# The last three blocks of a filter's forward transform as three fp16 products instead of one fp32 product

## The chip, the cores and the metric

The kernel runs on one core of a Trainium2 chip. The metric is the device time of one execution in microseconds, as the median of several runs; the span is the time from the first to the last instruction of one profiled execution.

## What is computed

Two parts share the core, and their results stand side by side in the output. A is attention with 16 heads of 28 columns and one key and value head (2048 rows, 448 columns). B is a global filter: a real two-dimensional FFT, a product with a complex weight, and the way back.

```
q = (x @ wq).reshape(B, S, 16, 28);  k = x @ wk;  v = x @ wv        # S = 2048, D = 448
p = softmax(q k^T * 28 ** -0.5);     a = (p v) @ wo
X = rfft2(B_x);  X = X * (w_r + 1j * w_i);  b = irfft2(X, (S, D))
out = concatenate([a, b], -1)
```

## The kernel before

A planner orders the first 60 us (projections, keys, the first query tile, and blocks 0 to 3 of the filter's first part). Then comes the loop over the attention, 16 groups (a chunk of 512 rows, four heads) of 16 steps. A step is: TensorE makes two pairs of score tiles (`scores`, four fp16 matmuls of 32 rows for each tile), ScalarE exponentiates each pair in one instruction of 128x1024 (`p`), and TensorE multiplies the result with the values (`values`, four fp32 matmuls). Scores use three double banks of PSUM, the values' sums one of two further banks, in turn by group; `group_out` copies a group's sum out on VectorE and so frees its bank.

Everything else of TensorE is cut into units that `fill` puts between steps, into the bank of the two that the current group does not use: the filter's blocks 5 to 7, later the third part of the filter (`z_unit`, `y_unit`), and the output product (`w_unit`, L1196). The order is fixed when the program is built, by a clock that adds estimated durations (`clk`, `after(when, duration, function)`), so each engine's instructions stand in one row and an instruction that has to wait holds up all that stand behind it.

The filter's first part works on eight blocks q of 256 columns. For each: VectorE folds the input by sums and differences (`fold_part`: `late["x", q]` to `late["f", q]`, 113x1024); `late_features` multiplies with the cosines `cs1` (units q, p with p = 0, 1: 16 fp32 matmuls of 113 columns, L173), VectorE copies the result to `late["a", q]` (L1013); `late_points` multiplies with the twiddles `late["w", q]` (8 fp32 matmuls of 226 columns, L1026), VectorE copies to `bs` (L1035) and SP stores it (`t1`). Blocks 0 to 3 are done by the planner, the features of block 4 too; the points of block 4 and blocks 5 to 7 are late units of the loop. When the last is stored, `spectrum` loads all points of the spectrum back (X), and VectorE alone runs the 32-point transforms, the weights and the way back for some 200 us, which opens the third part.

Two numbers are needed on every partition as a scale: `bounce` stores a column of maxima to DRAM (`md`), loads it back broadcast to all partitions (`mw`), and after 14 us by the clock VectorE reduces `mw` and computes the scales. Before the change this happens twice: early for the values' and the output weight's scale (`largest`; `m`, `scales`), which the first `group_out` needs, and once for the filter's third part (`mx`). `weight_top` loads the filter's weight eight times for a maximum.

The tiles `spoh` and `spol` are the four spare tiles that hold the blocks' data until the output product needs them; `banks` is all of PSUM, `vs` the values, `ka` the keys, `qt`, `qh`, `ql`, `qd`, `qa` the query tile of the next group on its way through DRAM, `woh` and `wol` the high and low half of the output weight.

Of the kernel before, what the change touches and what calls it, by code (L numbers as in the profile page):

```python
# [12 lines left out]
F32 = mybir.dt.float32  # L13
# [88 lines left out]
def kernel(ctx: ExitStack, tc: tile.TileContext, t: dict):  # L102
# [29 lines left out]
    def spin(*dims):  # L132
        return view(bank[next(turn) % 6], *dims)
# [9 lines left out]
    for (n, q), x in late.items():  # L143
        dims = {"x": dict(k=4, n=256), "f": dict(k=4, j=4, h=2, m=32), "w": dict(h=2, j=4, m=64), "a": dict(j=2, e=2, n=226)}[n]
        late[n, q] = x.rearrange(f"p ({' '.join(dims)}) -> p {' '.join(dims)}", **dims)
    xb, ff = {}, {}
# [20 lines left out]
    def features(pa, f, p):  # L167
        for e in range(2):
            for k in range(2):
                for h in range(2):  # L170
                    for r in range(2):
                        r0 = 64 * h + 32 * r
                        mm(pa[r0:r0 + 32, e, 113 * k:113 * k + 113], f[:113, 2 * r + k, 2 * p + e, h], cs1[:113, 2 * r + k],  # L173
                           start=True, stop=True)
# [24 lines left out]
    def late_load(q, names):  # L199
        for n in names:  # L200
            nc.sync.dma_start(late[n, q], t["xb"][q] if n == "x" else t["fz"][:, q - L])
# [30 lines left out]
    with tc.tile_pool(name="f1", bufs=2) as f1[0], tc.tile_pool(name="w1", bufs=1) as w1, ExitStack() as ctx1:  # L232
# [234 lines left out]
        def late_start():  # L467
            late_load(5, "xw")
            late_load(6, "xw")
            late_load(4, "w")  # L470
# [148 lines left out]
        def tops():  # L619
# [115 lines left out]
    def after(when, dur, f, *a):  # L735
        heapq.heappush(events, (when, next(serial), dur, f, a))
# [172 lines left out]
    def bounce(m, then):  # L909
        d = dp.tile([128, 2], F32, name="md", bufs=2)  # L910
        nc.sync.dma_start(d, m[:, :2])
        w = ap.tile([128, 128, 2], F32, name="mw", bufs=1)
        nc.sync.dma_start(w, d.rearrange("(o a) b -> o a b", o=1).to_broadcast([128, 128, 2]))

        def go():
            V.tensor_reduce(m[:, :2], w.rearrange("p a b -> p b a"), axis=AX.X, op=ALU.max)
            V.tensor_scalar(m[:, :2], m[:, :2], 1e-30, None, op0=ALU.max)
            then(m)
        after(clk["dve"] + 14.0, 1.0, go)
# [75 lines left out]

    def late_fold(q, part=0):
        fold_part(late["x", q][:113], late["f", q][:113], part)
        if part < 2:
            after(clk["dve"], (1.22, 1.4)[part], late_fold, q, part + 1)
        else:  # L1000
            if q == 6:
                late_load(7, "x")
            work["l"].extend([late_features(q, 0), late_features(q, 1)])

    def late_features(q, p):
        def go(b):
            features(view(bank[b], 2, 226), late["f", q], p)
            after(clk["pe"] + LAG, 0.6, out, b)
            if q < 7 and p:
                after(clk["pe"] + (1.8 if q == 5 else 5.0), 1.22, late_fold, q + 1)  # L1010

        def out(b):
            V.tensor_copy(late["a", q][:, p], view(bank[b], 2, 226))  # L1013
            free[b] = clk["dve"] + 0.1
            after(clk["dve"] + 0.2, 0.0, work["l"].appendleft, late_points(q, p))
        return 0.86, go

    bsl = {}

    def late_points(q, p):  # L1020
        def go(b):
            pb = view(bank[b], 2, 226)
            for h in range(2):
                for e in range(2):
                    for m in (0, 32):
                        mm(pb[64 * e + m:64 * e + m + 32, h], late["w", q][:, h, 2 * p + e, m:m + 32], late["a", q][:, p, e],  # L1026
                           start=True, stop=True)
            after(clk["pe"] + LAG, 0.6, out, b)
            if q == 6 and p:
                late_load(7, "w")  # L1030

        def out(b):
            if p == 0:
                bsl[q] = fp.tile([128, 2, 2, 2, 113], F32, name="bs")
            V.tensor_copy(bsl[q][:, :, :, p], view(bank[b], 2, 2, 113))  # L1035
# [7 lines left out]
        return 0.76, go  # L1043
# [337 lines left out]
def _constants():  # L1381
# [41 lines left out]
    c["fw"], c["fz"] = fw[:, :16], fz.reshape(128, 4, 2, 4, 64)  # L1423
    c["fi"] = np.stack([rot(2 * np.pi * (np.outer(kp, n1) / 64 + n2 * kp[:, None] / S)) for n2 in range(32)], 1)
    c = {k: np.ascontiguousarray(v.astype(f)) for k, v in c.items()}
    for k, scale in (("fi", 64.0), ("cs3", 32.0 * D)):
        x = c[k] * f(scale)
        h = x.astype(np.float16)
        c[k] = np.ascontiguousarray(np.stack([h, (x - h.astype(f)).astype(np.float16)], 2))
# [68 lines left out]
```

## Time and profile before

| | |
|---|---|
| median of 3 runs (lowest, highest) | 579.97 us (579.77, 580.02) |
| the profiled execution: time, span | 579.57 us, 577.8 us |
| granted clock of TensorE | 1.0 |
| busy share of the span | TensorE 99%, ScalarE 89%, VectorE 68%, GpSimd 19% |

A line of a timeline has the start in us, the duration, the engine, the source line and the instruction with its output and inputs; a bracket at the end tells how long the engine stood idle before it and what ended that. Since matmuls are pipelined, a unit's own time on TensorE is the distance from its start to the start of what follows, not its shown duration. In a table by stretches each engine has its busy time and, in brackets, its instructions.

### The profile page before, as it was taken

What the parts mean: (1) busy time and instruction counts of PE and PEld (TensorE: products, weight loads), DVE (VectorE), ACT (ScalarE), POOL (GpSimd) and SP (SyncE); (2) the same over time, 40 slices, a digit from 0 to 9 for tenths busy, and PEclk for the clock granted to TensorE, in tenths of its full rate; (3) what the DMA queues carried; (4) which work ended last, traced back from release to release, by engine and by line L of the source; (5) the groups of instructions that cost most, each with busy time, mean ns of one, the idle gap of its engine ahead of it and who ended that gap; (6) DMA issues with size and microseconds to landing.
All of it is one profiled execution on the core that took longest, in us unless ns stands there. A gap on an engine that the chain in (4) does not pass through costs nothing.

```text
span 577.8 us, 20635 instructions
## 1 busy us (share of the span) xinstructions
PE 571.3 (99%) x8941; PEld 300.6 (52%) x8941; DVE 390.5 (68%) x747; ACT 513.3 (89%) x580; POOL 110.5 (19%) x199
## 2 busy tenths in 40 slices
PE   9999999999999999999999999999999999999997
PEld 7877454545554444444444444445455555555554
DVE  5996727955421999998998887854366743366544
ACT  4744899999999999999999999998999887899982
POOL 1023311212103012121201311123202321011110
PEclk9999999999999999999999999999999999999999
DMA  8864682625417102243301120457224341212111
GB/s 290 295 205 140 175 247 73 191 81 146 161 37 218 58 18 66 75 123 98 91 34 57 41 60 31 155 208 230 78 88 128 109 130 70 89 58 73 41 55 65
DMA packets 38502, 66.27 MB, mean 115 GB/s; under 512 B 7013, under 2 KB 28653, under 8 KB 38401
## 3 DMA queue, kind: packets, MB, share of 16 engines
q1 hardware_dynamic: 29576, 38.95, 21.1%
q0 software_dynamic: 8688, 25.76, 14.2%
q8 instruction: 70, 1.15, 0.8%
q14 instruction: 24, 0.19, 0.1%
q10 hardware_dynamic: 144, 0.23, 0.1%
HBM read 44.22 MB, written 19.97 MB: 111 GB/s over the span
## 4 chain that ended last, share of the span: by engine, by line
PE 72%; issue 7%; DVE 5%; DMA 3%; POOL 2%; ACT 0%; POOLq 0%; DVEq 0%; ACTq 0%
PE banks L1258 31%; PE banks L1277 30%; PE banks L1196 6%; PE banks L1094 2%; PE banks L1120 2%; DMA rd<-rs 1%; DMA wf<-w 1%; DVE X L817 1%; DVE X L818 1%; PE banks L1026 1%; POOL R L1164 1%; DVE X L859 1%; PE banks L173 0%; ACT yb L1208 0%; DVE w L852 0%
## 5 line engine op out<-in xcount | busy, mean ns | idle before, releaser
L1261 ACT ACTIVATE p<-banks 128x1024 f32<-128x1024 f32 x512 | 477.2, 1094 | 23.7 <-PE banks L1258 22.3
L1258 PE MATMUL banks<-qa,ka 128*32 128x512 f16 x4096 | 276.4, 379 | 0.4 <-PEq L646 0.4
L1277 PE MATMUL banks<-p,vs 128*32 128x512 f32 x2048 | 268.6, 592 | 0.0
L1258 PEld LDWEIGHTS <-ka 128*32 128x32 f16 x4096 | 129.5, 96 | 167.1 <-issue 119.1
L1277 PEld LDWEIGHTS banks<-p,vs 128*32 128x32 f32 x2048 | 69.9, 110 | 43.5 <-issue 1.7
L1156 POOL DMA_DIRECT2D sd<-qraw x15 | 10.1, 671 | 165.4 <-DVE qraw L1151 165.4
L1196 PE MATMUL banks<-woh,o 128*32 128x448 f16 x464 | 39.6, 353 | 0.1
L1164 POOL DMA_DIRECT2D R<-rd x60 | 30.8, 521 | 38.3 <-DMA rd<-rs 38.1
L1196 PEld LDWEIGHTS <-o 128*32 128x32 f16 x720 | 22.6, 97 | 27.4 <-issue 20.2
L859 DVE SCALAR_TENSOR_TENSOR X<-w,X 128x226 f32<-128x226 f32 (+2 forms) x72 | 34.1, 474 | 2.4
L1151 DVE TENSOR_SCALAR qraw<-banks,scales 128x512 f32<-128x512 f32 x15 | 11.3, 750 | 31.5 <-PE banks L1277 31.4
L1201 DVE TENSOR_SCALAR ya<-banks,scales 128x448 f32<-128x448 f32 x12 | 8.2, 683 | 27.5 <-PE banks L1196 27.5
L1127 DVE TENSOR_SCALAR w<-banks,scales 128x256 f32<-128x256 f32 x16 | 7.7, 484 | 27.3 <-PE banks L1120 27.3
L1162 POOL DMA_DIRECT2D rd<-rs x15 | 8.2, 549 | 90.1 <-DVE rs L1161 81.6
L1196 PE MATMUL banks<-wol,o 128*32 128x448 f16 x256 | 24.4, 352 | 0.0
L340 PE MATMUL banks<-xh,wqh 128*128 128x512 f32 x64 | 23.6, 399 | 0.0
L340 PE MATMUL banks<-xh,wql 128*128 128x512 f32 x64 | 23.0, 390 | 0.0
L344 ACT ACTIVATE qraw<-banks 128x512 f32<-128x512 f32 x16 | 9.3, 595 | 15.0 <-PE banks L340 15.0
L817 DVE TENSOR_TENSOR X<-X 128x904 f32<-128x904 f32 (+2 forms) x10 | 9.1, 906 | 16.1 <-DMA X<-t 16.1
L852 DVE SCALAR_TENSOR_TENSOR w<-X 128x113 f32<-128x113 f32 (+2 forms) x56 | 17.8, 356 | 0.1
L1035 DVE COPY bs<-banks 128x452 f32<-128x452 f32 x8 | 5.0, 619 | 18.6 <-PE banks L1026 18.5
L340 PE MATMUL banks<-xl,wqh 128*128 128x512 f32 x48 | 17.3, 390 | 0.0
(157 smaller groups left out, 553.1 us busy)
## 6 DMA issues: line engine op xcount, KB each, us to landing
qa<-qd SPq DMA_DIRECT2D x62, 128.0 KB
ob<-yo SPq DMA_DIRECT2D x16, 256.0 KB
t<-bs SPq DMA_DIRECT2D x16, 226.0 KB
w<-w POOLq DMA_DIRECT2D x8, 452.0 KB, 4.7
X<-t POOLq DMA_DIRECT2D x8, 452.0 KB, 7.1
wf<-w POOLq DMA_DIRECT2D x8, 452.0 KB, 4.0
x<-t POOLq DMA_DIRECT2D x8, 452.0 KB, 4.4
R<-rd POOLq DMA_DIRECT2D x60, 56.0 KB, 2.1
```

The source lines that it names most:

```text
L340: mm(pq[c, g], w[:, j, gs], x[:, j], start=(j == 0 and n == 0), stop=(j == 3 and n == 1))
L817: todo(226 * n, lambda: TT(both(a), both(a), both(b), op=ALU.add), at)
L852: STT(out, y, sy, x, op0=ALU.mult, op1=ALU.add if c > 0 else ALU.subtract)
L859: todo(226 * n, lambda d=d, q=q: STT(both(d), t[0].rearrange("p r n f -> p r (n f)"), q, both(a), op0=ALU.mult, op1=ALU.add))
L1094: mm(pz[r, j], fb["c2", q % 2][:, x, e, j, r], fb["fi", q % 2][:, j, f], start=(n == 0), stop=(n == 2))
L1120: mm(py[m:m + 32, k].rearrange("p (j n) -> p j n", j=4), cs3[:w, kind, f, m:m + 32], fb["z", q % 2, e][:w, x, :, 64 * r:64 * r + 64], star ...
L1151: V.tensor_scalar(o, bank[b], scale_v, None, op0=ALU.mult)
L1164: nc.gpsimd.dma_start(R[32 * i:32 * i + DH], rd[i:i + 1].to_broadcast([DH, CW]))
L1196: mm(p[r:r + 32], x[c][:, g, s][:, r:r + 32], w[:, m], start=(g == 0 and n == 0), stop=(g == NG - 1 and n == 2))
L1258: mm(bank[b + h][r], ka[:, k:k + 32], qa[c, g][:, 2 * p + h], start=True, stop=True)
L1261: nc.scalar.activation(pt[i], banks[:, b:b + 2], AF.Exp, scale=SCALE / UP / UP)
L1277: mm(bank[b][32 * i:32 * i + 32], vs[:, kc], pt[2 * st + i // 2][:, i % 2], start=(kc == 0), stop=(kc == 15))
```

## The change

Blocks 5 to 7 are computed as three fp16 products: the folded input and the feature result are each split into a high and a low fp16 half, scaled first, and the cosines and twiddles come from DRAM already scaled and split (`cs16`, `fz16`). High by high, high by low and low by high are summed in PSUM. A unit of `late_features` has 48 fp16 matmuls instead of 16 fp32 ones, a unit of `late_points` 24 instead of 8.

The scale of a block comes from its largest input. `late_top` reduces the three raw inputs to `mt` (three columns) and sends them through a `bounce` of their own (`md3`, then `mw` with 384 columns; the same buffer serves the bounce of `largest`, which now stands behind it). `fix` makes `tops[q]` (t5, t6, t7) from it, and `late_split` (two VectorE instructions of 113x1024) stands between the fold and the features. The copy of a feature result becomes two instructions (high, low), the copy of the points gets a factor.

Block 7 gets two tiles of its own (`x7`, `W7`) that are loaded at the loop's start together with `cs16`, instead of waiting for block 6 to be done with its. `weight_top` starts at 14 instead of 24 on the clock. In the planner's part the task `fm_task(3)` (L183 before) now stands before the first transposes of the values, and the last feature unit of block 4 is cut in two around the load of a register (`values_load`).

```
-        late["x", q], late["f", q] = one[:, :1024], one[:, 1024:]
-        late["w", q], late["a", q] = two[:, o:o + 512], two[:, o + 512:o + 1416]
+        if q < 7:
+            late["x", q], late["W", q] = one[:, :1024], two[:, o:o + 512]
+        late["f", q], late["A", q] = one[:, 1024:], two[:, o + 512:o + 1416]
+    late["C", 0] = spare[1][1][:, :452]
...
+        fm_task(3)
         tv = add(PE, 0.6, first_values, users[-6], ident_, *krow_, *fetched["v"][:7])
         users.append(None)
-        fm_task(3)
...
+            pas[4, 1] = spin(2, 226)
+            features(pas[4, 1], ff[4], 1, (0,))
             small["rv"] = nc.values_load(bits.bitcast(I32)[0:1, 0:1])
-            pas[4, 1] = spin(2, 226)
-            features(pas[4, 1], ff[4], 1)
+            features(pas[4, 1], ff[4], 1, (1,))
...
+        d = dp.tile([128, cols], F32, name=f"md{cols}", bufs=2)
+        nc.sync.dma_start(d, m[:, :cols])
+        w = view(ap.tile([128, 384], F32, name="mw", bufs=1), 128, cols)
+        nc.sync.dma_start(w, d.rearrange("(o a) b -> o a b", o=1).to_broadcast([128, 128, cols]))
...
+        after(clk["dve"] + 14.0, 1.0 if cols < 3 else 3.0, go)
...
+    def late_top(qs):
+        m = ap.tile([128, 8], F32, name="mt", bufs=1)
+        V.memset(m, 0.0)
+        for n, q in enumerate(qs):
+            V.tensor_reduce(m[:113, n:n + 1], late["x", q][:113], axis=AX.XY, op=ALU.max, apply_absolute_value=True)
+        def fix(m):
+            for n, q in enumerate(qs):
+                tops[q] = ap.tile([128, 2], F32, name=f"t{q}", bufs=1)
+                V.tensor_scalar(tops[q][:, 1:2], m[:, n:n + 1], 1.0 / ROW, None, op0=ALU.mult)
+                V.reciprocal(m[:, 4:5], m[:, n:n + 1])
+                V.tensor_scalar(tops[q][:, 0:1], m[:, 4:5], 4096.0, None, op0=ALU.mult)
+                if q in folded:
+                    after(clk["dve"], 0.75, late_split, q, 0)
+        bounce(m, fix, 3)
...
+    def late_split(q, n):
+        f, x, scale = late["f", q][:113], late["F", q][:113], tops[q][:113, 0:1]
+        if n == 0:
+            V.tensor_scalar(x[:, 0], f, scale, None, op0=ALU.mult)
+            after(clk["dve"], 1.25, late_split, q, 1)
+        else:
+            STT(x[:, 1], f, scale, x[:, 0], op0=ALU.mult, op1=ALU.subtract)
             work["l"].extend([late_features(q, 0), late_features(q, 1)])
+    THREE = (0, 0), (0, 1), (1, 0)
...
-            V.tensor_copy(late["a", q][:, p], view(bank[b], 2, 226))
+            V.tensor_scalar(a[:, 0], pa, k, None, op0=ALU.mult)
+            STT(a[:, 1], pa, k, a[:, 0], op0=ALU.mult, op1=ALU.subtract)
...
-    after(24.0, 0.0, weight_top, 0)
+    after(14.0, 0.0, weight_top, 0)
     work["l"].extend([late_points(4, 0), late_points(4, 1)])
-    after(3.0, 1.22, late_fold, 5)
-    total = 12 * 2.09 + 32 * 0.67 + 6 * 0.86 + 8 * 0.76
+    late_load(0, "C")
+    for n, size in (("x", 1024), ("W", 512)):
+        shaped(n, 7, ap.tile([128, size], F32, name=n + "7", bufs=1))
+        late_load(7, n)
+    after(6.0, 3.4, late_top, (5, 6, 7))
+    after(6.1, 1.22, late_fold, 5)
+    total = 12 * 2.09 + 32 * 0.67 + 6 * (0.64 + 0.58) + 2 * 0.76
```

SP's row at the start of the loop, before: the keys' second half (`ka`), the query tile of the next group (`qd`, `qa`), and the bounce of `largest`.

```order
L499 DMA ka<-ka 32x1024 x2
L215 DMA qd<-qh 128x512
L215 DMA qd<-ql 128x512
L218 DMA qa_79<-qd 32x4x512 x4
L911 DMA md<-m 128x2
L913 DMA mw<-md 128x256
```

The same place now:

```order
L510 DMA ka<-ka 32x1024 x2
L212 DMA spol<-cs 128x904
L212 DMA x_976<-xb 128x1024
L212 DMA W_978<-fz 128x1024
L226 DMA qd<-qh 128x512
L226 DMA qd<-ql 128x512
L229 DMA qa_79<-qd 32x4x512 x4
L923 DMA md_1092<-mt 128x3
L925 DMA mw<-md_1092 128x384
L923 DMA md_1158<-m 128x2
L925 DMA mw<-md_1158 128x256
```

Three loads stand ahead of the query tile, and the bounce of `largest` stands behind the new one.

VectorE's row ahead of the first `group_out` (the row that writes `qraw` from `banks`), before, from the reduction of `mw` on; seven small instructions of the scales are left out between the two pieces:

```order
L916 TENSOR_REDUCE m<-mw 128x2
L917 TENSOR_SCALAR m<-m 128x2
```

```order
L768 TENSOR_SCALAR woh<-wo,scales 128x448
L770 SCALAR_TENSOR_TENSOR wol<-wo,scales,woh 128x448
L893 TENSOR_REDUCE peaks<-w 128x1
L1151 TENSOR_SCALAR qraw<-banks,scales 128x512
```

Now the reduction of the new bounce stands first, with ten small instructions behind it, then the following, and behind the second reduction the nine small ones as before:

```order
L905 TENSOR_REDUCE peaks<-w 128x1
L1041 TENSOR_SCALAR spoh<-spoh,t_1357 113x1024
L928 TENSOR_REDUCE m<-mw 128x2
```

```order
L1044 SCALAR_TENSOR_TENSOR spoh<-spoh,t_1357 113x1024
L780 TENSOR_SCALAR woh<-wo,scales 128x448
L782 SCALAR_TENSOR_TENSOR wol<-wo,scales,woh 128x448
L218 TENSOR_SCALAR qt<-qraw,mask,cvec 128x512
L219 CAST qh<-qt 128x512
L220 TENSOR_TENSOR ql<-qt,qh 128x512
L1216 TENSOR_SCALAR qraw<-banks,scales 128x512
```

`group_out` has the split of block 5 and the next query tile ahead of it, and two bounces instead of one.

TensorE's row at the first late feature unit that uses the bank which that `group_out` frees. Before it stands after the 17th values step (two score pairs, values, the unit):

```order
L1258 LDWEIGHTS ka
L1258 MATMUL banks<-qa_79,ka 32x512
L1277 MATMUL banks<-p,vs 32x512 x4
L173 MATMUL banks<-spol,spoh 32x113 x16
L1258 LDWEIGHTS ka
```

Now it is the first late feature unit of all, after the 18th values step, with a weight load ahead of each matmul (48 pairs):

```order
L1323 LDWEIGHTS ka
L1323 MATMUL banks<-qa_79,ka 32x512
L1342 MATMUL banks<-p,vs 32x512 x4
L1058 LDWEIGHTS spoh
L1058 MATMUL banks<-spol,spoh 32x113
```

Counted in values steps, the feature and points units of blocks 5 to 7 stood after steps 7 to 53 and now stand after steps 18 to 51; the two points units of block 4 stay after steps 0 and 4. From there on the units of the loop stand within one or two steps of where they were.

More of the change, by code (lines that the diff above doesn't have):

```diff
@@ L165, with features @@
     at1 = {}
-    def features(pa, f, p):
-        for e in range(2):
+    def features(pa, f, p, es=(0, 1)):
+        for e in es:
             for k in range(2):
@@ L200, in late_load @@
         for n in names:
-            nc.sync.dma_start(late[n, q], t["xb"][q] if n == "x" else t["fz"][:, q - L])
+            src = t["xb"][q] if n == "x" else t["fz16"][:, q - L - 1] if n == "W" else t["fz" if n == "w" else "cs16"]
+            nc.sync.dma_start(late[n, q], src)
     qa, qd = {}, {}
@@ L1003, in late_fold @@
             work["l"].extend([late_features(q, 0), late_features(q, 1)])
+    THREE = (0, 0), (0, 1), (1, 0)
     def late_features(q, p):
         def go(b):
-            features(view(bank[b], 2, 226), late["f", q], p)
-            after(clk["pe"] + LAG, 0.6, out, b)
+            pa, f, c = view(bank[b], 2, 226), late["F", q], late["C", 0]
+            for e in range(2):
+                for k in range(2):
+                    for n, (x, y) in enumerate(THREE):
+                        for h in range(2):
+                            for r in range(2):
+                                r0 = 64 * h + 32 * r
+                                mm(pa[r0:r0 + 32, e, 113 * k:113 * k + 113], f[:113, x, 2 * r + k, 2 * p + e, h],
+                                   c[:113, 2 * r + k, y], start=(n == 0), stop=(n == 2))
+            after(clk["pe"] + LAG, 1.3, out, b)
@@ L1009, in go @@
             if q < 7 and p:
-                after(clk["pe"] + (1.8 if q == 5 else 5.0), 1.22, late_fold, q + 1)
+                after(clk["pe"] + 1.8, 1.22, late_fold, q + 1)
         def out(b):
-            V.tensor_copy(late["a", q][:, p], view(bank[b], 2, 226))
+            a, pa = late["A", q][:, p], view(bank[b], 2, 226)
+            k = 2.0 ** -17
+            V.tensor_scalar(a[:, 0], pa, k, None, op0=ALU.mult)
+            STT(a[:, 1], pa, k, a[:, 0], op0=ALU.mult, op1=ALU.subtract)
             free[b] = clk["dve"] + 0.1
-            after(clk["dve"] + 0.2, 0.0, work["l"].appendleft, late_points(q, p))
@@ L1016, in late_features, with late_ready @@
-        return 0.86, go
-    bsl = {}
+            after(clk["dve"] + 0.2, 0.0, late_ready, q, p)
+        return 0.64, go
+    def late_ready(q, p):
+        work["l"].insert(len(points), late_points(q, p))
+        points.append((q, p))
+    bsl, points = {}, []
     def late_points(q, p):
         def go(b):
+            if q > L:
+                points.remove((q, p))
             pb = view(bank[b], 2, 226)
             for h in range(2):
[L1024 to L1027, printed above, removed]
+                for n, (x, y) in enumerate(THREE if q > L else ((0, 0),)):
+                    for e in range(2):
+                        for m in (0, 32):
+                            w, a = ((late["W", q][:, h, x], late["A", q][:, p, y]) if q > L else
+                                    (late["w", q][:, h], late["a", q][:, p]))
+                            mm(pb[64 * e + m:64 * e + m + 32, h], w[:, 2 * p + e, m:m + 32], a[:, e],
+                               start=(n == 0), stop=(n == 2 or q == L))
@@ L1034, in out @@
                 bsl[q] = fp.tile([128, 2, 2, 2, 113], F32, name="bs")
-            V.tensor_copy(bsl[q][:, :, :, p], view(bank[b], 2, 2, 113))
+            y, pb = bsl[q][:, :, :, p], view(bank[b], 2, 2, 113)
+            if q > L:
+                V.tensor_scalar(y, pb, tops[q][:, 1:2], None, op0=ALU.mult)
+            else:
+                V.tensor_copy(y, pb)
             free[b] = clk["dve"] + 0.1
@@ L1042, in out @@
                     after(clk["dve"] + 0.1, 0.0, spectrum)
-        return 0.76, go
+        return 0.58 if q > L else 0.76, go
     def spectrum():
```

42 lines of the change are left out of this document (23 added, 19 removed).

## The prediction

> **What bounds the kernel now.** I read the page's groups first: two engines carry the loop, ScalarE with the exponentials and TensorE.
>
> ```profile
> L1261 ACT ACTIVATE p<-banks 128x1024 f32<-128x1024 f32 x512 | 477.2, 1094 | 23.7 <-PE banks L1258 22.3
> L1277 PE MATMUL banks<-p,vs 128*32 128x512 f32 x2048 | 268.6, 592 | 0.0
> ```
>
> ScalarE is idle for only 23.7 us over the whole kernel, and nearly all of that is waiting for scores. Which of the two ends last differs by stage, so next the busy times by stretches (columns: PE, PEld, DVE, ACT, POOL):
>
> ```profile
> 62.00:180.00 118.00, 117.97 (x1804) 58.85 (x1804) 64.48 (x110) 114.22 (x124) 26.35 (x49) 1.00 0.49 139
> 180.00:220.00 40.00, 40.00 (x532) 16.66 (x528) 33.73 (x50) 40.00 (x45) 6.22 (x11) 1.00 0.24 85
> 220.00:380.00 160.00, 159.89 (x2308) 73.56 (x2304) 142.79 (x315) 159.06 (x173) 27.58 (x50) 1.00 0.25 78
> 380.00:562.00 182.00, 182.00 (x3496) 97.09 (x3492) 94.73 (x161) 163.51 (x174) 35.48 (x61) 1.00 0.32 104
> ```
>
> From 62 to 180 us ScalarE lacks 3.78 us: there the late units of the filter are on TensorE, and TensorE sets the end. From 180 to 220 ScalarE is full. From 380 on TensorE sets the end again, with work that the change does not touch. Whether shorter units shorten the time is thus read from 62 to 180. The timeline of ScalarE and TensorE there gives the step and the price of a unit:
>
> ```profile
> 146.01 15.69 ACT L1261 ACTIVATE p<-banks 128x1024 f32<-128x1024 f32 x17 [0.21 <-PE banks L1258]
> 158.72 1.05 PE L1258 MATMUL banks<-qa,ka 128*32 128x512 f16 x16
> 159.58 1.04 PE L1277 MATMUL banks<-p,vs 128*32 128x512 f32 x8
> 160.44 0.96 PE L173 MATMUL banks<-spol,spoh 113*32 113x113 f32 x32
> 161.22 1.48 PE L1258 MATMUL banks<-qa,ka 128*32 128x512 f16 x24
> 166.38 0.95 PE L1026 MATMUL banks<-spol 128*32 128x226 f32 x16
> 167.15 1.48 PE L1258 MATMUL banks<-qa,ka 128*32 128x512 f16 x24
> ```
>
> Exponentials follow each other at (15.69 - 1.09)/16 = 0.913 us, so a step of two takes ScalarE 1.825 us. On TensorE it takes 160.44 - 158.72 = 1.72. A step thus leaves TensorE 0.105 us for units. A feature unit takes 161.22 - 160.44 = 0.78 us, a points unit 0.77. In the stretch are 6 and 8 of them, 10.8 us, in about 65 steps that have room for 6.8; the difference of 4.0 is close to the 3.78 that ScalarE lacks. So each microsecond taken from the units there is one off the end, up to 3.8.
>
> **The units themselves.** The trace has two fp16 units of the same build, with a weight load for each matmul, on four column strips of the array: 48 matmuls of 128 columns and 24 of 256.
>
> ```profile
> 414.41 0.86 PE L1094 MATMUL banks<-fi,c 128*32 128x128 f16 x48
> 415.08 1.05 PE L1258 MATMUL banks<-qa,ka 128*32 128x512 f16 x16
> 425.45 0.84 PE L1120 MATMUL banks<-z,cs 112*32 112x256 f16 x24
> 426.11 0.62 PE L1258 MATMUL banks<-qa,ka 128*32 128x512 f16 x8
> ```
>
> They take 0.67 and 0.66 us. The new feature unit is 48 of 113 columns: between 0.67 x 113/128 = 0.59 (columns count) and 0.67 (pairs count). I take 0.61, nearer the first, because half the pairs at twice the columns cost the same. A saving of 0.17 each, 6 x 0.17 = 1.0 us (0.7 to 1.1). The points unit, 24 of 226: 0.66 x 226/256 = 0.58 to 0.66; I take 0.58, a saving of 0.19, 6 x 0.19 = 1.1 us (0.7 to 1.1). The points of block 4 stay fp32.
>
> The Trainium skill (TensorE: Matmul & The Clock Gate, "Back-to-back issue gap") has a rule against this: a stream of weight load and matmul with 128 columns takes about 81 ns a matmul. By that 48 pairs would be 3.9 us instead of 0.78, and the six feature units alone would cost 18.7 us. The row of 48 pairs in 0.67 us, 14 ns each, speaks against it here, since four strips work side by side.
>
> **The planner's part.** TensorE stands idle for 0.41 us ahead of the last feature unit before the loop, behind the register load:
>
> ```profile
> 59.87 0.98 PE L173 MATMUL banks<-spol,f 113*32 113x113 f32 x32 [0.41 <-issue]
> ```
>
> Half a feature unit (0.39) now stands ahead of the load, and the points of block 3 earlier. Between 0 and 0.4 us, I take 0.2. The order of the rest is the same; what ScalarE evicts comes no later.
>
> **What moves on SP, GpSimd and VectorE.** Three loads (226, 512 and 256 KB) go into SP's row ahead of the query tile and its bounce; two of them leave later places. This is the busiest part for the DMA engines. SP's row there and the loads of GpSimd, with the second bounce for comparison (a start, a duration, the issue):
>
> ```profile
> 63.94 1.23 SPq L499 DMA_DIRECT2D ka<-ka  x2
> 71.90 1.75 SPq L218 DMA_DIRECT2D qa<-qd  x4
> 74.03 0.34 SPq L911 DMA_DIRECT2D md<-m  x1
> 85.74 0.34 SPq L913 DMA_DIRECT2D mw<-md  x1
> 169.45 0.50 SPq L911 DMA_DIRECT2D md<-mx  x1
> 174.10 0.34 SPq L913 DMA_DIRECT2D mw<-md  x1
> 71.38 0.54 POOL L898 DMA_DIRECT2D w<-w  x1 [5.13 <-DVE m L782]
> w<-wo POOLq DMA_DIRECT2D x2, 448.0 KB, 5.2
> 71.00:85.00 14.00, 14.00 (x224) 6.90 (x220) 3.93 (x7) 13.58 (x16) 3.70 (x7) 1.00 0.85 256
> SPq L913 <- DMA md<-m: 11.3, 1, 11.3
> ```
>
> The store of 1 KB took 11.7 us in the loads' traffic (74.03 to 85.74), later 4.65. VectorE then:
>
> ```profile
> 78.48 0.63 DVE L1013 COPY spol<-banks 128x452 f32<-128x452 f32 x1 [4.06 <-PE banks L173]
> 86.19 0.63 DVE L1035 COPY bs<-banks 128x452 f32<-128x452 f32 x1 [7.08 <-PE banks L1026]
> 89.05 0.44 DVE L916 TENSOR_REDUCE m<-mw 128x2 f32<-128x256 f32 x1 [2.23 <-DMA mw<-md]
> 91.04 0.45 DVE L768 TENSOR_SCALAR woh<-wo,scales 128x448 f16<-128x448 f32 x1
> 92.12 1.08 DVE L893 TENSOR_REDUCE peaks<-w 128x1 f32<-128x904 f32 x1
> 94.75 0.75 DVE L1151 TENSOR_SCALAR qraw<-banks,scales 128x512 f32<-128x512 f32 x1 [1.54 <-PE banks L1277]
> 95.41 0.54 DVE L207 TENSOR_SCALAR qt<-qraw,mask,cvec 128x512 f32<-128x512 f32 x1
> 97.06 0.45 DVE L768 TENSOR_SCALAR woh<-wo,scales 128x448 f16<-128x448 f32 x1
> L1080 DVE TENSOR_SCALAR c<-x,scales 128x904 f16<-128x904 f32 x8 | 5.5, 690 | 9.5 <-PE banks L1094 9.5
> L1081 DVE SCALAR_TENSOR_TENSOR c<-x,scales,c 128x904 f16<-128x904 f32 x8 | 9.3, 1159 | 0.7
> ```
>
> Added to VectorE before the first `group_out`: three reductions of 1024 columns (1.08 x 1024/904 = 1.2 each), a reduction of the new `mw`, ten small ones of 0.2, and a split (0.69 and 1.16 at 904 columns; 0.75 and 1.25 here): 8.5 us. Its idle 4.06 + 7.08 + 2.23 us in that place, of which the first two go because the units they waited for come later, would hide them; the later two splits and six low halves of about 0.63 lie in the 53.5 us that VectorE is idle between 62 and 180. What does not hide is the path through the two bounces, and TensorE waits at its end: the first late feature unit, after the 18th values step, needs the bank that `group_out` frees. When it would be there:
>
> - `x7` is issued behind the keys and `cs16`, about 66.0 (65.17 and two issues), and lands about 71.2 if it takes the 5.2 of the 448 KB loads beside it.
> - Its reduction ends about 72.5. `md3` stands behind the four loads of `qa`. With 1.0 MB more ahead at 256 GB/s (3.9 us), partly into idle, its issue moves from 74.03 to about 75.5.
> - `md3` takes 4.65 to 11.7 us. GpSimd's loads, which made it 11.7, start when the reductions of `m` are done (71.38), and these now stand behind `x7`, some 4 us later; so `md3` gets part of its way ahead of them. I take 7.5: `mw` is issued at 83.0 (80.2 to 87.2) and lands 3.3 later (85.74 to 89.05), at 86.3.
> - From there VectorE needs 0.6 + 2.0 (small ones) + 1.1 (`peaks`) + 0.75 + 2.0 (second reduction and scales, 89.05 to 91.04) + 1.25 + 1.1 (92.12 - 91.04) + 1.65 (query tile, 95.41 to 97.06) + 0.7 = 11.2 us, and the second bounce runs beside the first part of it. `group_out` ends about 97.5 (94.7 to 101.7).
>
> TensorE arrives there when 36 exponentials are done and the 18th values have run: 62.75 (start of the first) + 36 x 0.913 + 0.9 = 96.5, with ScalarE's small lags about 96.8:
>
> ```profile
> 62.75 15.87 ACT L1261 ACTIVATE p<-banks 128x1024 f32<-128x1024 f32 x17 [1.29 <-PE banks L1258]
> ```
>
> So TensorE waits 0.7 us (0 to 4.9), and ScalarE, at most three banks behind, waits with it: this comes back nowhere.
>
> **The sum.** Against the profiled execution's 579.57 us: -1.0 (features) -1.1 (points) -0.2 (start) + 0.7 (the wait) = -1.6, so 577.97. The median of the runs is 0.40 above that execution: 578.4. The last late unit stands two steps earlier than before, so the chain from `spectrum` to the third part keeps its place, and the other stretches stay.
>
> **Rivals.** A difference of 0.2%, 1.16 us, is about what a measurement tells from none.
>
> First, the bounce comes later and eats the saving. The saving without the wait is 2.3; with a wait of 1.1 to 3.5 the time stays within 0.2%. For `mw` issued at 84.7, midway to the longest, `group_out` ends at 99.2, the wait is 2.4, the time 580.1. For it speaks the 11.3 us row; against it, that the loads' traffic starts later now.
>
> Second, slower: `md3` takes the whole 11.7 us, as the row of before has it. Then `mw` is issued at 87.2, `group_out` ends at 101.7, TensorE waits 4.9 and the time is 582.6. It decides from a wait of 3.5 us on, `mw` issued at about 85.8. Against it: half of `qa`, which `md3` stands behind, can pass before GpSimd's loads begin.
>
> Third, the fp16 units cost more than the old ones, because the weight load ahead of each matmul sets the pace. One load takes 97 ns on its own:
>
> ```profile
> L1094 PEld LDWEIGHTS <-c 128*32 128x32 f16 x576 | 12.9, 97 | 6.2 <-issue 4.8
> ```
>
> If only four ran side by side and nothing else overlapped, a pair would be 24 ns and a feature unit 48 x 24 = 1.16 us; six would cost 2.3 us more than now, and with the other terms the time is 579.57 + 2.3 - 1.1 - 0.2 + 0.7 + 0.4 = 581.7. The 14 ns for a pair in the units with these very loads say no. The rule of the Trainium skill's same section, a floor of about 25 ns for each short matmul, points the same way as this rival; no sum here uses it.
>
> **How the numbers follow.** The wait under 1.1 us, and faster: 0.47. First rival: 0.30. Second: 0.21. Third: 0.02. Faster, within, slower: 0.47, 0.30, 0.23. The low end is no wait with the largest savings: 1.1 + 1.1 + 0.4 = 2.6 and a little for ScalarE's lags, 577.2. The high end takes in half of the second rival, a wait of 3.9: 581.6. The likeliest case's own range is 577.2 to 578.8.
>
> **What would show it.** Right: the 48 matmuls of a late feature unit in about 0.61 us and the 24 of points in 0.58; ScalarE lacking less than 3.8 us between 62 and 180; `mw` issued before 84 and VectorE's first `qraw` from `banks` ended before 98. Wrong: a wait of TensorE of over 1 us ahead of the first late feature unit near 97 us, with the chain of waits going through `mw`, or units above 0.7 us.

## The result, and the profile after the change

The changed kernel takes 585.19 us (median of 6 runs, 583.71 to 586.87) against 579.87 (579.21 to 580.21) for the kernel before: a ratio of 1.0092 with an interval of 1.0071 to 1.0112. It is slower. Lines of the changed kernel have other numbers: scores L1323, values L1342, exponentials L1326, late features L1058, late points L1090, `group_out` L1216, `bounce` L923 and L925, its reduction L928, the first output unit L1261. The profiled execution took 586.87 us with a span of 585.1; 579.57 before, so 7.30 us are to be found. It is the slowest of the six, 1.7 us above their median, so the account below is that of the longest execution; the loss of the median is 5.3 us.

First three of the stretches of before (busy time of PE, PEld, DVE, ACT and POOL, then the granted clock and DMA):

```profile
62.00:180.00 118.00, 113.11 (x1869) 54.25 (x1873) 79.64 (x137) 108.78 (x118) 22.34 (x41) 0.97 0.48 136
180.00:220.00 40.00, 40.00 (x544) 17.19 (x540) 27.26 (x40) 40.00 (x45) 8.10 (x15) 1.00 0.30 101
220.00:380.00 160.00, 158.53 (x2268) 72.05 (x2264) 143.76 (x306) 157.05 (x171) 29.33 (x52) 1.00 0.24 71
```

From 62 to 180 us ScalarE now lacks 9.2 us where it lacked 3.8, and TensorE, which was never idle there, is idle for 4.9 at a mean clock of 0.97. From 220 to 380 TensorE has lost another 1.5. The timeline of TensorE shows the first place:

```profile
96.86 1.04 PE L1342 MATMUL banks<-p,vs 128*32 128x512 f32 x8
102.55 1.33 PE L1058 MATMUL banks<-spol,spoh 113*32 113x113 f16 x48 [4.65 <-DVE qraw L1216]
103.64 2.80 PE L1323 MATMUL banks<-qa,ka 128*32 128x512 f16 x24
106.20 1.94 PE L1342 MATMUL banks<-p,vs 128*32 128x512 f32 x8
107.91 0.88 PE L1058 MATMUL banks<-spol,spoh 113*32 113x113 f16 x48
137.78 0.80 PE L1058 MATMUL banks<-spol,spoh 113*32 113x113 f16 x48
138.39 1.49 PE L1323 MATMUL banks<-qa,ka 128*32 128x512 f16 x24
142.27 0.77 PE L1090 MATMUL banks<-spol 128*32 128x226 f16 x24
142.85 1.05 PE L1323 MATMUL banks<-qa,ka 128*32 128x512 f16 x16
```

The units have the predicted size: 138.39 - 137.78 = 0.61 us for features, 142.85 - 142.27 = 0.58 for points. But TensorE waits 4.65 us ahead of the first one, for the bank that `group_out` frees, and the unit behind the wait takes 103.64 - 102.55 = 1.09 us instead of 0.61, the 24 score matmuls 2.56 instead of 1.29. The stretches around it tell why (the third number from the right is the granted clock):

```profile
98.00:101.00 3.00, 0.00 (x0) 0.00 (x0) 2.93 (x5) 1.13 (x2) 0.00 (x0) 1.00 0.00 0
101.00:102.00 1.00, 0.00 (x0) 0.00 (x0) 0.96 (x3) 0.00 (x0) 0.00 (x0) 0.63 0.02 7
103.00:108.00 5.00, 5.00 (x75) 2.22 (x68) 2.75 (x4) 2.86 (x3) 2.53 (x5) 0.50 0.49 138
108.00:109.00 1.00, 1.00 (x60) 0.84 (x56) 0.16 (x1) 0.00 (x0) 0.00 (x0) 0.96 0.90 288
```

TensorE's last matmul ends at 97.9. Some 3.3 us later its clock falls to half (the mean of 0.63 from 101 to 102 puts this at 101.25), and it comes back only near 108.1, after 5.55 us of work. That work takes twice its time: 2.8 us more. The Trainium skill (TensorE: Matmul & The Clock Gate, "What's actually happening") says that the clock halves after an idle window of about 3.4 us and comes back after about as long a busy one; the trace agrees with the first (about 3.3), and the way back took 5.5 here.

What held `group_out` up, in SP's, GpSimd's and VectorE's rows and SP's waits:

```profile
76.81 0.38 SPq L923 DMA_DIRECT2D md<-mt  x1
76.82 0.54 POOL L910 DMA_DIRECT2D w<-w  x1 [10.74 <-DVE m L794]
78.93 2.12 POOL L814 DMA_DIRECT2D X<-t  x4
82.69 0.34 SPq L925 DMA_DIRECT2D mw<-md  x1
90.70 0.75 DVE L928 TENSOR_REDUCE mt<-mw 128x3 f32<-128x384 f32 x1 [8.43 <-DMA mw<-md]
91.62 0.32 SPq L925 DMA_DIRECT2D mw<-md  x1
95.85 0.43 DVE L928 TENSOR_REDUCE m<-mw 128x2 f32<-128x256 f32 x1 [1.32 <-DMA mw<-md]
101.75 0.75 DVE L1216 TENSOR_SCALAR qraw<-banks,scales 128x512 f32<-128x512 f32 x1
SPq L925 <- DMA md<-m: 8.0, 1, 8.0
SPq L925 <- DMA md<-mt: 5.4, 1, 5.4
```

The trip of `mt` through memory takes 90.70 - 76.81 = 13.9 us, beside GpSimd's loads (two of `w`, two of `wo`, four gathers of X, 3.2 MB), which start at the same moment. The second trip, of `m`, waits 8.0 us for its own store and lands at 95.85; `group_out` ends at 102.5.

The second place, near 230 us, is the first output unit, which waits for the rows of `o` that come through memory:

```profile
227.43 1.16 PE L1323 MATMUL banks<-qa,ka 128*32 128x512 f16 x16
230.06 0.37 PE L1261 MATMUL banks<-woh,o 128*32 128x448 f16 x4 [1.47 <-DMA o<-lows]
```

For an account of the whole I took from the traces the start of the exponentials number 36, 60, 128, 180 and 511 (the last), counted from each kernel's own first one, number 0, and subtracted that of the kernel before (us, minus is ahead; "rest" is what the start of the first exponential and the way from the last one to the end of the span add):

| kernel | 36 | 60 | 128 | 180 | 511 | rest |
|---|---|---|---|---|---|---|
| changed | -0.94 | +5.59 | +4.57 | +6.10 | +6.77 | +0.53 |
| bounces swapped | -0.94 | -1.59 | -1.47 | -1.62 | -1.60 | +0.30 |
| loads past the bounces | -0.28 | -0.97 | -2.63 | -2.31 | -2.71 | +1.50 |
| gathers alone past them | -0.96 | +0.43 | -0.27 | -0.34 | +0.29 | +0.75 |
| late units as before, loads moved | -0.01 | -0.01 | +4.58 | +4.32 | +3.20 | +1.42 |
| output units later | -0.85 | -1.54 | -2.95 | -3.53 | -1.17 | +1.11 |

In the changed kernel 6.5 us go between the 36th and the 60th exponential, the wait and the slow clock less the savings in between; 1.5 more go between the 128th and the 180th although units there are cheaper too. 6.77 + 0.53 = 7.30.

### The profile page after: what moved, and what is told of

Same layout as the page of the kernel before. It is cut to its first block, busy times and chain, and to the rows that moved or that the text cites. A ratio compares the mean times of both kernels' runs of the same rounds, so it can differ in the third digit from the quotient of the medians.

```text
span 585.1 us, 20948 instructions
## 1 busy us (share of the span) xinstructions
PE 572.5 (98%) x9085; PEld 295.6 (51%) x9085; DVE 405.5 (69%) x774; ACT 513.0 (88%) x580; POOL 110.6 (19%) x199
## 3 DMA queue, kind: packets, MB, share of 16 engines
q1 hardware_dynamic: 30008, 39.38, 20.7%
## 4 chain that ended last, share of the span: by engine, by line
PE 81%; DMA 5%; DVE 1%; issue 1%; ACT 1%; SPq 1%; POOL 0%; ACTq 0%; DVEq 0%
PE banks L1323 35%; PE banks L1342 35%; PE banks L1261 6%; DMA mw<-md 2%; PE banks L1159 2%; PE banks L1185 2%; DMA qd<-qh 1%; DMA md<-mt 1%; PE banks L1058 1%; PE banks L1090 1%; SPq L229 1%; DMA o<-lows 0%; ACT yb L1273 0%; DVE spoh L1044 0%; ACT p L1326 0%
## 5 line engine op out<-in xcount | busy, mean ns | idle before, releaser
L1326 ACT ACTIVATE p<-banks 128x1024 f32<-128x1024 f32 x512 | 476.8, 1097 | 30.9 <-PE banks L1323 30.4
L1323 PE MATMUL banks<-qa,ka 128*32 128x512 f16 x4096 | 276.8, 381 | 0.4 <-PEq L658 0.4
L1342 PE MATMUL banks<-p,vs 128*32 128x512 f32 x2048 | 267.9, 594 | 0.0
L1323 PEld LDWEIGHTS <-ka 128*32 128x32 f16 x4096 | 126.3, 96 | 172.5 <-issue 127.3
L1342 PEld LDWEIGHTS banks<-p,vs 128*32 128x32 f32 x2048 | 68.2, 110 | 44.8 <-issue 2.2
L1261 PE MATMUL banks<-woh,o 128*32 128x448 f16 x464 | 39.5, 353 | 1.5 <-DMA o<-lows 1.5
L1261 PEld LDWEIGHTS <-o 128*32 128x32 f16 x720 | 21.7, 97 | 28.4 <-issue 20.1
L1216 DVE TENSOR_SCALAR qraw<-banks,scales 128x512 f32<-128x512 f32 x15 | 11.2, 750 | 20.9 <-PE banks L1342 20.9
L1261 PE MATMUL banks<-wol,o 128*32 128x448 f16 x256 | 24.1, 352 | 0.0
L355 ACT ACTIVATE qraw<-banks 128x512 f32<-128x512 f32 x16 | 9.3, 596 | 15.1 <-PE banks L351 15.0
L945 DVE TENSOR_TENSOR w<-X,wf 128x904 f32<-128x904 f32 x16 | 17.0, 1096 | 0.2
```

Of the source, the lines that this page charges most:

```text
L945: TT(u[r], both(s), wt[k][:, r:r + 1].to_broadcast([128, 2, 452]), op=ALU.mult)
L1216: V.tensor_scalar(o, bank[b], scale_v, None, op0=ALU.mult)
L1261: mm(p[r:r + 32], x[c][:, g, s][:, r:r + 32], w[:, m], start=(g == 0 and n == 0), stop=(g == NG - 1 and n == 2))
L1323: mm(bank[b + h][r], ka[:, k:k + 32], qa[c, g][:, 2 * p + h], start=True, stop=True)
L1326: nc.scalar.activation(pt[i], banks[:, b:b + 2], AF.Exp, scale=SCALE / UP / UP)
L1342: mm(bank[b][32 * i:32 * i + 32], vs[:, kc], pt[2 * st + i // 2][:, i % 2], start=(kc == 0), stop=(kc == 15))
```

## The experiments

The theories: W, the loss is TensorE's wait ahead of the first late feature unit, made by two bounces in the traffic of loads; C, the clock doubles what the wait costs; G and then H, what makes the wait near 230; S, the edits ahead of the loop; U, the rival, that the fp16 units and VectorE's added work cost the time wherever they stand.

**The bounces swapped.**

```
-    after(6.0, 3.4, late_top, (5, 6, 7))
+    after(11.0, 3.4, late_top, (5, 6, 7))
...
-        after(clk["dve"] + 14.0, 1.0 if cols < 3 else 3.0, go)
+        after(clk["dve"] + (14.0 if cols < 3 else 20.0), 1.0 if cols < 3 else 3.0, go)
```

> The changed kernel with the two bounces in the other order: the scale of the output (m) goes through memory first, the largest inputs (mt) after it and past the first group_out. Theory W (the loss is TensorE's wait ahead of the first late feature unit, 5.7 us and some 2 us of refilling behind it, because group_out stands behind both bounces): group_out ends at 96 to 98 instead of 102.5, the wait at the first late feature unit (now three values steps later) falls to 0 to 2.5 us, and the time to 579.5 (578 to 581.5). Theory G (a further 2 us are lost near 230 us, because GpSimd's gathers stand ahead of the small store rd): here R's loads stand ahead of the four gathers again, so that wait goes as well and the time is nearer 578. Theory U (the fp16 units and VectorE's added work cost the time wherever they stand): 585.

579.38 us, ratio 0.9996 (0.9987 to 1.0005). (The 5.7 us of the expectation is ScalarE's wait behind the late unit; TensorE's own is the 4.65 shown.) Its rows of `m`'s trip and of `group_out`:

```profile
75.44 0.84 SPq L923 DMA_DIRECT2D md<-m  x1
86.24 0.34 SPq L925 DMA_DIRECT2D mw<-md  x1
90.55 0.42 DVE L928 TENSOR_REDUCE m<-mw 128x2 f32<-128x256 f32 x1 [10.40 <-DMA mw<-md]
95.25 0.74 DVE L1216 TENSOR_SCALAR qraw<-banks,scales 128x512 f32<-128x512 f32 x1
```

The trip is as slow as before (15.1 us), but there is only one of them ahead of `group_out`, which ends at 96.0. TensorE waits nowhere in the loop. All the units, splits and low halves are still there: theory U, a cost wherever they stand, is out. But the first late feature unit now stands after the 21st values step instead of the 18th and starts at 103.0, later than the 102.5 at which `group_out` ended in the changed kernel; so this run alone does not tell the order of the bounces from the place of the unit. The run with the gathers alone, below, does. The waits of ScalarE for scores from 62 to 180 us, kernel before and then this one:

```profile
ACT p L1261 <- PE banks L1258: 4.1, 10, 1.3
ACT p L1326 <- PE banks L1323: 2.5, 6, 1.3
```

The 1.6 us between them are what the fp16 units are worth in this trace, and they stay to the last exponential (-1.60). The traced execution (578.26) is the fastest of ten, though; the median is only 0.3 below that of the kernel before, measured beside it (579.66), so a gain is not shown.

**GpSimd's loads moved past the bounces.**

```
-        after(30.0 + i, 0.0, spread, i)
-    after(34.0, 0.0, first_points)
-    after(14.0, 0.0, weight_top, 0)
+        after(44.0 + i, 0.0, spread, i)
+    after(48.0, 0.0, first_points)
+    after(34.0, 0.0, weight_top, 0)
...
-            after(clk["dve"] + 8.5, 0.0, weight_top, k + 1)
+            after(clk["dve"] + 6.5, 0.0, weight_top, k + 1)
```

> The changed kernel with GpSimd's loads of the weights' largest and the first four gathers of X moved some 15 to 20 us later, past both bounces; the bounces stay in their order. Theory W with its cause in the DMA traffic: the 192 KB load of mw takes 3 to 4 us instead of 8, the store md about 4.6; group_out ends near 95, the first late feature unit (which the plan now sets five values steps earlier) waits 0 to 2 us, and the time is 579.5 (578 to 581.5). If the bounces are slow without that traffic too: mw still 8 us, 584 to 587. Theory U: 585. Theory G: the wait of about 2 us near 230 stays, since a gather still stands ahead of rd.

578.59 us, ratio 0.9985 (0.9976 to 0.9995). The trip of `mt` in this kernel:

```profile
77.78 0.38 SPq L923 DMA_DIRECT2D md<-mt  x1
81.38 0.34 SPq L925 DMA_DIRECT2D mw<-md  x1
84.68 0.77 DVE L928 TENSOR_REDUCE mt<-mw 128x3 f32<-128x384 f32 x1 [1.27 <-DMA mw<-md]
95.47 0.75 DVE L1216 TENSOR_SCALAR qraw<-banks,scales 128x512 f32<-128x512 f32 x1 [0.44 <-PE banks L1342]
```

6.9 us instead of 13.9, and now `group_out` waits for the values, not they for it. (The plan also sets the first late feature unit five values steps earlier here.) The Trainium skill (DMA: Bandwidth & Descriptors, "Queues, rings and completion order") says that each DMA engine takes turns, packet by packet, between the queues that have work for it. Only a part of that is seen here: in the changed kernel the store of `mt` landed while GpSimd's loads ran on (`mw` was issued at 82.69, the loads' last packets ended at 90.45), but the load of `mw` was in use only at 90.70, when they had ended, and in the kernel before the store itself took until their end (85.20; `mw` issued at 85.74).

**A fixed scale, no trip of `mt` at all.**

```
-        bounce(m, fix, 3)
+        V.memset(m, 64.0)
+        after(clk["dve"] + 14.0, 0.5, fix, m)
```

> The changed kernel with a fixed scale for the three late blocks: the reductions of the largest inputs, the splits and the fp16 units stay, and only the trip of mt through memory is left out, so the scale does not follow the inputs. Theory W: one bounce is left, group_out ends near 96, no wait above 1 us ahead of a late feature unit, time 578 to 580 (less with theory G's part, if its wait goes too). Theory U: 584 to 585, since all the work of TensorE and all but one small reduction of VectorE's stay.

580.37 us, ratio 1.0004 (0.9995 to 1.0013), with no wait above 1 us; the loss of the changed kernel is gone, but nothing of the units' saving is left. In the trace TensorE stands idle for 0.78 us near 91 for a reason that it does not show, its first score came 0.65 later than in the kernel before, and the way from the last exponential to the end took 1.7 longer; why, was not followed up.

**The edits ahead of the loop alone**, in the kernel before: `fm_task(3)` ahead of `tv`, and `features(pas[4, 1], ff[4], 1, es)` once ahead of `values_load` and once behind.

> The kernel before with only the two edits ahead of the loop: the points of block 3 planned earlier, and the last feature unit cut in two around the register load. Theory S (these edits cost the 0.35 us by which the loop began later): the first score near 62.2 instead of 61.9 and the time 0.3 longer than before, 580.2. As the prediction had it: 0.2 shorter, 579.7. If the later start comes from the added loads instead: no difference, 579.9.

579.74 us, ratio 1.0004 (0.9995 to 1.0013): nothing. TensorE still stands idle behind the register load, for 0.49 us, with the half unit ahead of it. The first score came at 62.07 instead of 61.87. In the kernel with these edits undone (below) it came at 62.64, later than in any other, so the start differs by some tenths for reasons that are not these edits.

**The wait filled with idle matmuls.** Ahead of the first late feature unit:

```
+            if (q, p) == (5, 0):
+                cg, gg, _ = steps[si // 2]
+                for m in range(48):
+                    r = slice(32 * (m % 4), 32 * (m % 4) + 32)
+                    mm(bank[2 * (2 * si % 3)][r], ka[:, r], qa[cg, gg][:, 0], start=True, stop=True)
```

> The changed kernel with 48 idle matmuls of 512 columns ahead of the first late feature unit, written into the score banks that are used next and overwritten there; each engine's order stays otherwise. They fill the first 2 to 3 us of the wait. Theory C (after the wait of 4.65 us TensorE's granted clock was 0.50 from 101.2 to 108.1, so that 5.5 us of work took twice its time): the wait still ends near 102.5, the unit behind it takes 0.6 instead of 1.1 us, and the time falls by 2.5 to 2.8, to 582.5. If the slow scores and values behind the wait have another cause (the transfers of that moment, the refilling of ScalarE): 585, or more by what the idle matmuls cost.

583.93 us (583.41 to 584.40), ratio 1.0078 (1.0063 to 1.0094). The unit behind the wait, and the stretches:

```profile
97.83 2.78 PE L1056 MATMUL banks<-qa,ka 128*32 128x512 f16 x48
100.56 0.80 PE L1063 MATMUL banks<-spol,spoh 113*32 113x113 f16 x48
101.17 1.49 PE L1328 MATMUL banks<-qa,ka 128*32 128x512 f16 x24
100.00:102.00 2.00, 2.00 (x76) 1.31 (x72) 1.97 (x4) 0.10 (x1) 0.59 (x1) 1.00 0.50 147
102.00:104.00 2.00, 1.67 (x35) 0.64 (x28) 1.76 (x3) 2.00 (x3) 0.00 (x0) 1.00 0.49 159
```

The unit takes 0.61 us, and the clock stays at 1.00. That fits theory C, but does not test it: the trip of `mt` took 12.2 us in this trace, `group_out` ended at 100.5 instead of 102.5, and the gap that the idle matmuls fill is 2.73 us, shorter than any that was seen to cost the clock. The 2.8 us of half clock are read from the changed kernel's own trace. The time fell by 1.3 us, half of what was expected: with TensorE back in time a points unit waits 1.01 us for the copy that frees its bank, and the third late feature unit 0.91 us for its split, waits that the longer one had covered (a larger one of this kind is shown below, in the run with the gathers alone). More traces bound the idle time that costs the clock: 0.96 us (the next run) and 1.74 us (the gathers alone) did not, with 1.00 behind them; 3.00 us did (the run with the stages on X later):

```profile
101.09 0.80 PE L1058 MATMUL banks<-spol,spoh 113*32 113x113 f16 x48 [3.00 <-DVE qraw L1216]
101.70 2.57 PE L1323 MATMUL banks<-qa,ka 128*32 128x512 f16 x24
102.00:104.00 2.00, 2.00 (x24) 0.90 (x20) 1.97 (x4) 1.33 (x2) 0.00 (x0) 0.50 0.61 190
```

Here the clock fell only when the unit was done, at 101.94, and was back at 105.36: 3.4 us at half, so 1.7 us lost. The length of the wait varies although the rows at this place do not: the trip through memory took 13.9, 12.4, 12.2 and 10.8 us in four traces in which they are the same (the changed kernel, the later stages on X, the idle matmuls, the next run). That the time of one kernel varies with it (583.71 to 586.87) is likely but not shown, as each kernel has one trace.

**The last gathers behind R.**

```
-            after(t0 + 1.0 * (i - 4), 0.0, spread, i)
+            after(t0 + 4.0 + 0.5 * (i - 4), 0.0, spread, i)
```

> The changed kernel with the last four gathers of X issued 2.5 to 4 us later in the plan, so that they stand behind rd and R in GpSimd's row as they did before the change. Theory G (rd, a small store, took 8.1 us beside two gathers, R and the other gathers were issued 10 us late, the norm of the group and the rows of o came late and TensorE waited 1.5 to 1.8 us ahead of the first output unit near 230): that wait is gone, time 583.4. If the wait near 230 only follows from the first one: it stays, 585.

585.51 us (583.49 to 587.53), ratio 1.0112 (1.0083 to 1.0140); TensorE still waits 0.89 us ahead of the first output unit (1.47 in the changed kernel). Theory G fell. The traced execution, 583.97, shows what is still lost without the long wait: the first late unit waits only 0.96 us, with no half clock behind it. In its place stand a half clock at the loop's start (about 1 us, last section), three waits of 0.3 to 0.9 us for VectorE's splits and copies, and 1.1 us outside the exponentials.

**Loads moved, gathers behind R, and the start's edits undone together.**

> Loads moved past the bounces (as in the run before), the last gathers behind R, and the two edits ahead of the loop undone: the fp16 units with every loss that the traces showed taken away. Theory W with theory G: no wait of TensorE above 0.3 us in the loop, its first exponential to its last 496 to 497.5 us instead of 499.7, and the time 577 to 578. Theory U has no part left in it: 580 or more would bring it back.

579.50 us, ratio 1.0011 (0.9999 to 1.0022). No wait at the late units, 3.2 us ahead at the 128th exponential, but 1.19 us of waiting at the first output unit, 0.8 lost by the later start and 1.3 behind the last exponential. The expectation was missed, and once more it is not theory G.

**The gathers alone past the bounces.** The first two pairs of lines of the edit of the loads, without `weight_top`.

> The changed kernel with only the first four gathers of X (1.85 MB) moved past both bounces; the 1.4 MB of weight loads stay between, and VectorE's and TensorE's order up to the first late feature unit is that of the changed kernel. Theory W with the traffic as cause, by its amount: the trip of mt through memory, 13.9 us from the store's issue to the load's end with 3.2 MB beside it and 6.9 with none, takes about 10; group_out ends near 98.5, the wait at the first late feature unit is 0.5 to 2 us, the clock stays up, and the time is 580 (579 to 582). If it is the first loads alone, whatever their amount: 13 to 14 us and 585.

580.55 us, ratio 1.0014 (1.0005 to 1.0023). The trip of `mt`, `group_out`, the first late feature unit and the wait of the third:

```profile
75.00 1.16 SPq L923 DMA_DIRECT2D md<-mt  x1
80.08 0.34 SPq L925 DMA_DIRECT2D mw<-md  x1
84.82 0.74 DVE L928 TENSOR_REDUCE mt<-mw 128x3 f32<-128x384 f32 x1 [2.95 <-DMA mw<-md]
96.20 0.75 DVE L1216 TENSOR_SCALAR qraw<-banks,scales 128x512 f32<-128x512 f32 x1
97.34 0.80 PE L1058 MATMUL banks<-spol,spoh 113*32 113x113 f16 x48
104.44 0.45 DVE L780 TENSOR_SCALAR woh<-wo,scales 128x448 f16<-128x448 f32 x1 [2.02 <-DMA wo<-wo]
115.68 0.69 PE L1058 MATMUL banks<-spol,spoh 113*32 113x113 f16 x40 [1.74 <-DVE spoh L1044]
```

9.8 us with 1.4 MB beside it. With at most one load it was 6.9 to 7.9 in four traces, with 3.2 MB 10.8 to 13.9 in four: the trip goes with the amount of traffic. Order and place are those of the changed kernel, the unit stands after the 18th values step, `group_out` ends at 96.95, and the first late unit no longer waits. So the wait is that of the bounces in the traffic. But the third waits 1.74 us for its split: VectorE lost 2.02 us to a late `wo` and has fold, split and low halves in one row. That much of theory U is right: VectorE's added work is hidden only as long as it runs in time.

**The stages on X 3 us later in the plan**, once with the loads moved and once in the changed kernel alone.

```
-        after(t0 + 7.0, 0.0, forward)
-        after(t0 + 7.0, 0.0, inverse)
+        after(t0 + 10.0, 0.0, forward)
+        after(t0 + 10.0, 0.0, inverse)
```

> The kernel with the loads moved past the bounces, and the stages on X (forward and inverse) begun 3 us later in the plan, so that 28 of their operations stand ahead of the eighth group's norm on VectorE instead of 32 (27 in the kernel before). Theory H (the wait of 0.6 to 1.8 us near 222 to 230 us comes from the plan: the late units end earlier in it than on the chip, so that more operations on X are written ahead of the norm, the rows of o come late and the first output unit waits): no wait of TensorE above 0.3 us there, and the time 0.6 to 1.0 below that kernel's 578.6, so 577.8. If the wait has another cause: it stays, 578.6. Theory U is out for this kernel either way if it stays below 579.

580.62 us, ratio 1.0026 (1.0009 to 1.0043): slower than with the loads moved alone. The wait at the first output unit stayed (0.63 us, 0.27 with the loads moved alone), as the next `group_out` and query tile now stood ahead of the norm, and 2.3 us more went between the 180th exponential and the last. A miss.

> The changed kernel with the stages on X begun 3 us later in the plan (28 operations ahead of the eighth group's norm instead of 32) and nothing else. Theory H: the wait of 1.77 us near 230 is gone, the wait at the first late feature unit stays, and the time is 1.5 to 2 below that of the changed kernel: 583.5 where TensorE's clock drops after the first wait, 582 where it doesn't. Theory G, with the gathers as the cause: the wait near 230 stays.

582.98 us, ratio 1.0059 (1.0045 to 1.0074), with the first late unit's wait still there (3.00). The first output unit follows what is ahead of it without a wait:

```profile
226.82 0.38 PE L1261 MATMUL banks<-woh,o 128*32 128x448 f16 x4
```

Theory H holds for the changed kernel: in its plan the late units end earlier, so VectorE's row has 32 operations on X ahead of the norm of the group where the kernel before has 27 (by the trace it is the fourth group, not the eighth: its norm starts at 224.1, before at 214.5); on the chip X came 20.7 us after the last points instead of 18.1, and the norm was late by both. Neither is enough alone: with the same 32 operations the wait was 1.47 us where X came 20.7 us after the last points, 1.19 at 20.4, 0.89 at 20.0, 0.27 at 19.7, and none at 18.7 (the idle matmuls). Why X comes later is open.

**The control: the kernel before with GpSimd's loads moved.**

> The kernel before with the same loads of GpSimd moved later, its fp32 units kept: whether the time of the kernel with moved loads belongs to the fp16 units or to the loads. Theory W (the loads matter only by the bounce, and before nobody waited for its end): 579.3 to 580, no difference. If the loads themselves were worth something: 578.6, and the fp16 units then bring nothing.

584.21 us, ratio 1.0078 (1.0066 to 1.0090). Up to the 60th exponential nothing changes (-0.01 in the table), so the moved loads bring no gain of their own there. Behind it this kernel makes a wait of its own, for a `group_out` behind late loads in VectorE's row, with the half clock after it (131.72 is the start of the feature unit that waits):

```profile
131.72 0.98 PE L173 MATMUL banks<-spol,spoh 113*32 113x113 f32 x32 [3.29 <-DVE qraw L1151]
```

For the total it is thus no control; for the first 60 exponentials it is.

**The first output units offered later**, with the loads moved: `after(clk["dve"] + 9.5, ...)` instead of 7.0 ahead of the `w_unit` list.

> The kernel with the loads moved past the bounces, and the first output units offered 9.5 instead of 7 us after the norm of the group in the plan, which puts the first of them two values steps later on TensorE (87 instead of 85) and changes nothing on VectorE. Theory H: the wait of 0.6 us near 222 is gone, and the time is 578.0 (577.4 to 578.6). If the units only meet another wait later: 578.6 or above, as the kernel with the later stages on X did. Theory U: 579.6 or more.

580.12 us, ratio 1.0007 (0.9999 to 1.0016). No wait is left in the loop, and the 180th exponential is 3.5 us ahead; 2.4 of it are lost by the last and 1.1 behind it. So the time did not follow the wait, and theory H's forecast for it was missed. Where these go I did not follow up.

## Why the prediction was wrong

**The units** came out as forecast: 0.61 and 0.58 us, 13 ns for a pair of load and matmul in the features; the third rival, with pairs of 24 ns, is out. Sized at 2.1 us together, they were worth 1.6 in the one trace with the bounces swapped, the order without any wait that is nearest to the kernel before, and 1.9 to 3.5 by the 180th exponential with the loads moved. Of that up to 2.4 were given back by the last exponential and 1.1 to 2.1 outside the exponentials, so most of it does not reach the time; where it goes is open.

**The start** was taken as -0.2; alone it measured nothing, as the idle time behind the register load stayed.

**The wait** is the step that failed: 0.7 us taken, 4.65 measured in the traced execution, within the ends of 0 to 4.9. It was wrong in the length of the trip: 10.8 us taken (7.5 for the store and the 3.3 of the kernel before for the load of `mw`), 13.9 measured. The store did better than taken, 5.9 us: `mw` was issued at 82.69, before the 84 that was named as a sign of being right. The load took 8.0. Its 3.3 in the kernel before came from a moment when the traffic was over; there the store had taken all of it. GpSimd's loads started together with the store (76.82 and 76.81), as the prediction's own figures say (71.38 and some 4 us, against 75.5), and not behind it. Starting later than before, they also ended later, at 90.45 instead of 85.20, and the load of `mw` was in use only then; what was counted in favour of the trip worked against it. In eight traces with all these loads beside it the first trip took 10.8 to 15.1 us, 2.9 to 11.7 for the store and 3.2 to 9.5 for the load: a store of some 3 us goes with a load of 7.8 to 9.5, a store of over 10 with one of 3.2 to 4.3.

Besides, the store left at 76.8 instead of 75.5, the second trip, "beside the first part of it", held VectorE for another 1.3 us, and VectorE's own work took 10.5 instead of 11.2. That makes 102.5 instead of 97.5 for the end of `group_out`; TensorE was there at 97.9 instead of 96.8.

**Missing from the sum:** the clock, put at nothing without a reason. The second rival had a wait of 4.9 us and the price of 582.6; with the 2.8 us of half clock that makes 585.4, near the 585.19 measured. That is in part luck: its mechanism, a store of 11.7 us, is not what happened (5.9), and the loss near 230 us is not in it. Without the clock its price was too low, and so was the high end of the range.

**"The other stretches stay"** was wrong by 1.5 us: the late units stand two steps earlier in the plan, but on the chip their last result was copied at 171.4 instead of 167.4, and the plan fills VectorE's row ahead of the norm by its own clock.

## What to carry to other kernels

A small trip through memory must be priced as one piece, in the traffic that will be beside it, and not by adding the legs of different moments; then ask which row stands behind it. In three traces a wait of TensorE of 3.0 to 4.65 us cost, on top of its own length, 1.7 to 2.8 us of half clock, and waits of up to 1.74 us did not, so a forecast with such a wait has a step in it. A new user of an existing queue or buffer is best put behind the one that others already wait for: the swap of the two bounces, which also set the first late unit three values steps later, gave back the whole loss.

## What the hardware showed that was not expected

The half clock is also seen with no long wait ahead of it: in two traces TensorE ran at 0.50 for 3.4 us at the start of the loop (61.9 to 65.3 with the loads past the bounces, 62.5 to 65.9 with the last gathers behind R). A row of the first:

```profile
63.00:64.00 1.00, 1.00 (x16) 0.45 (x12) 0.68 (x1) 0.76 (x1) 0.00 (x0) 0.50 0.28 84
```

No idle time of over 0.63 us stands in the 30 us ahead of it, and idle times of 0.4 to 0.5 stand at the same place in traces whose clock stayed at 1.00. The cause is open.

The best of all these is the kernel with the loads past the bounces, 0.15% below the kernel before (0.9985, 0.9976 to 0.9995). That is less than the 0.2% that the prediction took as the least a measurement tells from none, and the three kernels with the same loads moved and one or two edits more came out at 1.0007 to 1.0026. So a gain in time from the fp16 units is not established.
